# Attention with a gated MLP on one core: a new table of the order of instructions, with the activation table loaded by an early small exponential

## The chip, the cores and the metric

The kernel runs on one core of a Trainium2 chip. The metric is the device time of one execution in microseconds (us). All times of engines below are of one execution taken by the hardware profiler. PE is TensorE (its weight loads, which overlap its matmuls, are PEld), DVE is VectorE, ACT is ScalarE, POOL is GpSimd, SP is SyncE, which here only issues DMAs.

## What is computed

Attention of 4 batches with 12 heads, 448 positions and head dimension 64, with a causal mask and a softmax, and on its output, batch by batch, a gated MLP with a residual:

```python
scores = scale * np.matmul(q, k.transpose(0, 1, 3, 2))
scores = np.where(mask, -1000000000.0, scores)
scores = scores - np.max(scores, axis=-1, keepdims=True)
attn = np.exp(scores)
attn = attn / (np.sum(attn, axis=-1, keepdims=True) + 1e-09)
x = np.matmul(attn, v)                     # heads side by side: 448 x 768 per batch
h = x @ w_in                               # 768 x 1024
h = 0.5 * h * (1.0 + np.tanh(c * (h + 0.044715 * h ** 3)))
u, v = (h[..., :d_ff // 2], h[..., d_ff // 2:])
v_n = (v - mu) / np.sqrt(var + 1e-06) * g_ln
v_s = np.einsum('ts,bsd->btd', w_sg, v_n) + b_sg[None, :, None]
return x + (u * v_s) @ w_out
```

## The kernel before

**Attention** goes by pairs of heads, 24 pairs p, six to a batch. For each pair SP fetches queries and keys (tile qk, L424) and values (vraw, L516). PE makes the scores in two halves (`score(g)`, L431, tiles s, four PSUM banks for the two heads). DVE adds the mask and takes the row maxima (`mxs`, L446: s and ngm out of s and mask). ACT takes the exponentials with the maximum as bias and row sums on the side (L454: P out of s and ngm, ten instructions a pair, 64 to 448 columns wide). Three sets of P tiles, P_90, P_91 and P_92, and of row sums, sm_117 to sm_119, take turns over the pairs. Then P is transposed: for the first eight pairs on PE (L496, tiles tx and ty), with an eviction to B on ACT (L503) or DVE (L501); for the others on DVE (L484), with a DMA to B (L488). PE multiplies by the values (PV: L522, tile o), DVE scales by the reciprocal of the row sums (xt, L549; the reciprocal is L464 to L466 and goes through DRAM, L471 and L474), and ACT or POOL split the result into two rounded parts x (L555 to L560).

**MLP.** Per batch, PE makes the v half of the hidden layer in four chunks of positions (128, 128, 128 and 64 rows), then the u half, the product with w_sg over the four normalized chunks vn, and the product with w_out; all of these are L577, tiles m. The gelu is `gelu2` (L585 to L590, ACT and DVE in turn); the 64-row chunk has its two halves added first (L611, L613), then the normalization (L617 to L626) and the split into two parts (L630 and L631, for the 64-row chunk L635 on ACT and L636 on DVE, tile vn3). The gate is L669 to L676, the residual goes into res on POOL (L689) and is added to the last product on DVE (L702), from where SP stores it (L706, L710). In the last batch the last tile is added and stored in two halves of 224 columns.

**Weights** are fetched (L364, and L350 for w_sg) and split into two rounded parts on ACT, DVE and POOL (L366 to L374, L352, L353), beside the first batch. At the start seven matmuls on a cleared tile (L339) stand on PE.

**The order.** Each function records its operations with `od.add(engine, duration, function, reads, writes, ...)`. A table of 1883 numbers, `ORDER`, gives the order in which they are emitted; that sets the order of the instructions on each engine and on SP's queue, and in what turn buffers and banks go round. `plan` only makes sure that the table keeps the recorded dependencies; the durations and flags in the calls go into no instruction.

```python
    def plan(self):
        done = set()
        for n in ORDER:
            assert self.ops[n]["deps"] <= done
            done.add(n)
```

Operation 3 of the table is one exponential on a constant column (L330). The function of an exponential needs a table in ACT, and the load (ACT_TABLE_LOAD) is put before the first exponential that ACT is given; before the change that is one of the scores' (L454), and operation 3 stands after operation 1208.

Of the kernel before, what the change touches and what calls it, by code (L numbers as in the profile page):

```python
# [12 lines left out]
AF = mybir.ActivationFunctionType  # L13
ALU = mybir.AluOpType
# [211 lines left out]
def attention_gated_mlp(ctx: ExitStack, tc: tile.TileContext, qk, vP, w_in, g_ln, w_sgT, b_sg, w_out, out):  # L226
    nc = tc.nc
# [4 lines left out]
    DH = DF // 2  # L232
# [533 lines left out]
```

## Time and profile before

| | before |
|---|---|
| median of 3 runs | 339.13 us (338.38 to 340.37) |
| profiled execution, its own time | 337.29 us |
| its span, first to last instruction | 335.5 us |
| PE busy | 324.1 us |
| DVE busy | 251.0 us |
| ACT busy | 208.5 us |
| POOL busy | 175.9 us |
| mean granted clock of PE | 0.994 |

The profiled execution's own time is 1.84 us under the median of the runs, and its span 1.8 us under its own time. Busy times are sums over the whole span; where an engine stands still has to be read from windows of the span, from the timeline, and from what ended each pause, which the trace gives in brackets. PE's ends are modelled, so a busy PE is not PE at its peak. An instruction's duration overlaps the next one's on ACT and DVE by some tenth of a microsecond, so that the cost of one in a row of many is the time from its start to the next start.

### The profile page before, as it was taken

The numbers are of one execution on the slowest core, as the hardware profiler recorded it, in microseconds if no ns is written. First come the engines' busy times: TensorE is split into PE (matmuls) and PEld (weight loads), VectorE is DVE, ScalarE is ACT, GpSimd is POOL, SyncE is SP. The second block draws the span as 40 slices with busy tenths as digits, with TensorE's granted clock in tenths as the row PEclk, the third lists the DMA queues.
The fourth block names the chain that finished last, engine by engine and source line by source line (L and its number), as shares of the span: only waits on it lengthen the run. The fifth ranks groups of instructions, "written<-read, shape, count | busy, mean of one in ns | idle before, by whom it ended". The sixth has DMA issues, their size and how long they took to land.

```text
span 335.5 us, 7568 instructions
## 1 busy us (share of the span) xinstructions
PE 324.1 (97%) x2590; PEld 266.3 (79%) x2591; DVE 251.0 (75%) x762; ACT 208.5 (62%) x674; POOL 175.9 (52%) x225
## 2 busy tenths in 40 slices
PE   5699999999999999999999999999999999999995
PEld 3467678768887987878888978878989987889994
DVE  4899898999999888967977597889788531644613
ACT  1999999999894637666784526486674302355210
POOL 4258766888986964020535942014256824132691
PEclk9899999999999999999999999999999999999999
DMA  7889968595583688638747858739437440010004
GB/s 227 312 247 307 277 218 267 177 288 160 130 265 103 178 215 235 197 98 226 217 127 214 229 150 204 195 95 243 101 104 206 91 159 3 0 55 2 18 36 164
DMA packets 30965, 56.55 MB, mean 169 GB/s; under 512 B 6096, under 2 KB 15056, under 8 KB 30928
## 3 DMA queue, kind: packets, MB, share of 16 engines
q1 hardware_dynamic: 30928, 56.08, 57.5%
q8 instruction: 20, 0.33, 0.4%
q14 instruction: 17, 0.14, 0.1%
HBM read 33.39 MB, written 5.90 MB: 117 GB/s over the span
## 4 chain that ended last, share of the span: by engine, by line
PE 93%; ACT 4%; DMA 1%; DVE 1%; issue 0%; ACTq 0%; DVEq 0%
PE m L577 65%; PE o L522 13%; PE s L431 11%; ACT P L454 3%; PE ty L496 2%; PE tx L496 2%; DMA qk<-in_qk_dram 1%; PE m L339 0%; ACT L454 0%; ACT vn L366 0%; ACT B L503 0%; DVE s L446 0%; DVE res L702 0%; DVE ngm L446 0%; ACTq L454 0%
## 5 line engine op out<-in xcount | busy, mean ns | idle before, releaser
L454 ACT ACTIVATE P<-s,ngm 128x320 f32<-128x320 f32 (+3 forms) x240 | 102.7, 460 | 28.1 <-DVE ngm L446 19.7
L446 DVE CUSTOM_DVE_ANT_0 s<-s,mask 64x64 f32<-64x64 f32 (+3 forms) x192 | 77.6, 435 | 7.5 <-PE s L431 5.8
L577 PE MATMUL m<-win,x 128*128 128x512 f32 (+1 forms) x264 | 65.9, 399 | 0.0
L577 PE MATMUL m<-g,wout 128*128 128x448 f32 x288 | 61.1, 367 | 0.0
L577 PE MATMUL m<-x,win 128*128 128x448 f32 x288 | 61.1, 367 | 0.0
L577 PEld LDWEIGHTS m<-x,win 128*128 128x128 f32 x288 | 53.9, 188 | 5.0
L577 PEld LDWEIGHTS m<-g,wout 128*128 128x128 f32 x288 | 53.9, 188 | 5.0
L577 PEld LDWEIGHTS m<-win,x 128*128 128x128 f32 (+1 forms) x264 | 47.4, 183 | 11.7
L454 ACT ACTIVATION_READ_ACCUMULATOR P<-s,ngm 128x1 f32 (+1 forms) x240 | 55.1, 233 | 0.0
L431 PE MATMUL s<-qk 64*64 64x64 f32 (+5 forms) x768 | 45.2, 371 | 5.0 <-DMA qk<-in_qk_dram 4.4
L431 PEld LDWEIGHTS s<-qk 64*64 64x64 f32 x768 | 30.7, 139 | 21.6 <-issue 8.5
L522 PE MATMUL o<-B,vraw 128*64 128x64 f32 (+4 forms) x672 | 45.0, 291 | 0.0
L522 PEld LDWEIGHTS o<-B,vraw 128*64 128x64 f32 x672 | 32.8, 137 | 12.7 <-issue 4.5
L484 DVE STREAM_TRANSPOSE P<-P 128x1024 f32<-128x1024 f32 x32 | 38.2, 1224 | 0.7 <-DMA B<-P 0.6
L577 PE MATMUL m<-wsg,vn 128*128 128x448 f32 x176 | 38.3, 369 | 0.0
L621 POOL TENSOR_TENSOR mv<-mv,mhalf 128x1 f32<-128x1 f32 (+1 forms) x16 | 10.0, 626 | 49.0 <-DVE mv L619 40.7
L577 PEld LDWEIGHTS m<-wsg,vn 128*128 128x128 f32 x176 | 32.6, 188 | 3.6 <-DVE vn L636 0.4
L558 POOL TENSOR_TENSOR x<-xt,x 128x448 fp32r<-128x448 f32 x24 | 27.5, 1148 | 14.5 <-ACT x L557 14.2
L702 DVE TENSOR_TENSOR res<-m,res 128x448 f32<-128x448 f32 (+1 forms) x25 | 14.8, 603 | 23.2 <-PE m L577 15.2
L586 DVE SCALAR_TENSOR_TENSOR tmp<-tmp,m 128x448 f32<-128x448 f32 (+1 forms) x28 | 17.9, 640 | 16.2 <-ACT tmp L585 16.0
L673 POOL TENSOR_TENSOR tmp<-tmp,g 128x448 f32<-128x448 f32 x16 | 18.3, 1152 | 18.8 <-DVE tmp L669 18.8
L585 ACT ACTIVATE tmp<-m 128x448 f32<-128x448 f32 (+1 forms) x28 | 15.5, 562 | 20.3 <-PE m L577 19.2
(76 smaller groups left out, 410.8 us busy)
## 6 DMA issues: line engine op xcount, KB each, us to landing
B<-P SPq DMA_DIRECT2D x64, 256.0 KB
qk<-in_qk_dram SPq DMA_DIRECT2D x24, 448.0 KB
vn<-in_w_in_dram SPq DMA_DIRECT2D x12, 512.0 KB
vraw<-in_vP_dram SPq DMA_DIRECT2D x24, 256.0 KB
rb<-rd SPq DMA_DIRECT2D x24, 224.0 KB
out_dram<-res SPq DMA_DIRECT2D x9, 448.0 KB
g<-in_w_out_dram SPq DMA_DIRECT2D x16, 192.0 KB
out_dram<-res SPq DMA_DIRECT2D x5, 224.0 KB
```

Source lines behind the costliest of these rows:

```text
L431: nc.tensor.matmul(out=s[z][bk].t[64 * h:64 * h + 64, col:col + n], lhsT=qk_.t[r, 0, q0:q0 + 64], rhs=qk_.t[r, 1, k0:k0 + n], start=True, ...
L446: nc.vector.tensor_tensor_reduce(out=o, in0=i, in1=mk, scale=-0.125, scalar=3e38, op0=ALU.add, op1=ALU.min, accum_out=ngm[ib[z]][c][0:m])
L454: act(n, lambda c=c, m=m, k0=k0, n=n, bk=bk, col=col, off=off, kc=kc, i=i, z=z: nc.scalar.activation(out=P[i][0:m, off:off + n], in_=s[z][ ...
L484: dve(PW, lambda z=z: nc.vector.transpose(A[ia][:, :, :, z, :].rearrange("p g t k -> p t g k"), P[ib[z]]), Pk[z] + [kp], Ak, 1.105)
L496: nc.tensor.transpose(out, P[ib[z]][:, col:col + 128], ident)
L522: nc.tensor.matmul(out=dst(o.t[r]), lhsT=vr.t[:, c, r], rhs=src(z), start=first and n == 0, stop=last and n == len(lst) - 1)
L558: pool_tt(S, lambda: nc.gpsimd.tensor_tensor(out=y.t[:, S + 64:], in0=x.t, in1=f(y.t)[:, 0:S], op=ALU.subtract), [x, y], [(y, 1)])
L577: nc.tensor.matmul(out=ps.t[0:l().shape[1], 0:n], lhsT=l(), rhs=rr(), start=(k == 0), stop=(k == len(mms) - 1))
L585: act(n, lambda: nc.scalar.activation(out=z(), in_=h(), func=AF.Square), [ps], [t])
L586: dve(n, lambda: nc.vector.scalar_tensor_tensor(out=z(), in0=z(), scalar=1.0 / GC, in1=h(), op0=ALU.add, op1=ALU.mult), [ps], [t])
L673: pool_tt(S, lambda z=z, u=u: nc.gpsimd.tensor_tensor(out=z(), in0=z(), in1=u.t, op=ALU.mult), [u], [t])
L702: dve(hi - lo, lambda rr=rr, ps=ps, z=z, lo=lo, hi=hi: nc.vector.tensor_tensor(out=rr.t[:, z, lo:hi], in0=ps.t[:, lo:hi], in1=rr.t[:, z, l ...
```

## The change

The set of instructions stays the same. What differs is the order, and arguments that only the planner reads: the exponentials of the scores are recorded as readers of the early exponential on a constant (so that this stands ahead of all of them in any table that `plan` accepts), some durations are longer, and the 64-row gelu and L636 carry a flag `port`.

```diff
 ORDER = (
-    84, 85, 86, 1, 4, 0, 2, 89, 87, 90, 96, 88, 95, 98, 91, 92, 97, 99, 93, 94, 125, 126, 128, 127, 12, 18, 13, 103,
...
+    2, 4, 1, 0, 3, 84, 125, 332, 12, 18, 166, 330, 24, 85, 89, 87, 90, 96, 88, 95, 98, 97, 86, 91, 93, 92, 99, 94,
...
-    od.add("act", 0.2, lambda: nc.scalar.activation(out=pad[:, 0:1], in_=mhalf, func=AF.Exp), ["sm0"], ["table"])
+    od.add("act", 1.35, lambda: nc.scalar.activation(out=pad[:, 0:1], in_=mhalf, func=AF.Exp), ["sm0"], ["table"])
...
-                    [s[z][bk], ("ngm", i, c), kp, ks] + ([("P", i, k - 1)] if k == 1 else [("P", i, 2)] if k == 4 else []),
+                    [s[z][bk], ("ngm", i, c), kp, ks, "table"] + ([("P", i, k - 1)] if k == 1 else [("P", i, 2)] if k == 4 else []),
...
-        od.add("dve", 0.42, inv, sk + [ks], [("rT", ip)])
+        od.add("dve", 0.573, inv, sk + [ks], [("rT", ip)])
...
-            tensor=rd[ip].tensor, offset=rd[ip].offset, ap=[[512, 8], [0, 16], [1, S]])), [("rd", ip)], [rb], 320e3, dur=0.56)
+            tensor=rd[ip].tensor, offset=rd[ip].offset, ap=[[512, 8], [0, 16], [1, S]])), [("rd", ip)], [rb], 360e3, dur=0.56)
...
-    def gelu2(ps, m, n, dst=None):
+    def gelu2(ps, m, n, dst=None, port=False):
...
-                                                      op1=ALU.mult), [ps], [t])
+                                                      op1=ALU.mult), [ps], [t], port=port)
...
-                                                      op0=ALU.add, op1=ALU.mult), [ps, t], [d])
+                                                      op0=ALU.add, op1=ALU.mult), [ps, t], [d], port=port)
...
-                t, z = gelu2(hs, m, DH)
+                t, z = gelu2(hs, m, DH, port=True)
...
-            od.add("dve", 0.07, lambda mv=mv, m=m: nc.vector.tensor_scalar(
+            od.add("dve", 0.125, lambda mv=mv, m=m: nc.vector.tensor_scalar(
...
-                out=z(), in_=z(), func=AF.Identity, scale=mv.t[0:m, 1:2], bias=mv.t[0:m, 2:3]), [mv], [t], True)
+                out=z(), in_=z(), func=AF.Identity, scale=mv.t[0:m, 1:2], bias=mv.t[0:m, 2:3]), [mv], [t], True, 2)
...
-                                                                 op=ALU.subtract), [t, y], [(y, 1)])
+                                                                 op=ALU.subtract), [t, y], [(y, 1)], port=True)
```

ACT from its first instruction, before and after. A row is line, operation, output and inputs with their shape; P_90 and sm_117 belong to pair 0, P_91 and sm_118 to pair 1, ngm_93 to ngm_100 are pair 0's maxima:

```order
L454 ACT_TABLE_LOAD
L454 ACTIVATE P_90,sm_117<-s,ngm_100 128x448
L454 ACTIVATE P_90,sm_117<-s,ngm_96 128x448
L454 ACTIVATE P_90,sm_117<-s,ngm_97 64x64
L454 ACTIVATE P_90,sm_117<-s,ngm_93 64x64
L454 ACTIVATE P_90,sm_117<-s,ngm_95 128x320
L366 ACTIVATE vn<-vn 128x512
L454 ACTIVATE P_90,sm_117<-s,ngm_94 64x64
L454 ACTIVATE P_90,sm_117<-s,ngm_94 128x128
L454 ACTIVATE P_90,sm_117<-s,ngm_98 128x128
L454 ACTIVATE P_90,sm_117<-s,ngm_99 128x320
L454 ACTIVATE P_91,sm_118<-s,ngm_104 128x448
```

```order
L330 ACT_TABLE_LOAD
L330 ACTIVATE pad<-mhalf 128x1
L454 ACTIVATE P_90,sm_117<-s,ngm_100 128x448
L454 ACTIVATE P_90,sm_117<-s,ngm_96 128x448
L454 ACTIVATE P_90,sm_117<-s,ngm_97 64x64
L454 ACTIVATE P_90,sm_117<-s,ngm_93 64x64
L454 ACTIVATE P_90,sm_117<-s,ngm_95 128x320
L454 ACTIVATE P_90,sm_117<-s,ngm_94 128x128
L454 ACTIVATE P_90,sm_117<-s,ngm_94 64x64
L454 ACTIVATE P_90,sm_117<-s,ngm_99 128x320
L454 ACTIVATE P_90,sm_117<-s,ngm_98 128x128
L454 ACTIVATE P_90,sm_117<-s,ngm_98 64x64
```

The table load now belongs to the exponential of L330, on the column pad, and the ten exponentials of pair 0 follow without a weight split (L366) between them; in the whole of the first two pairs one L366 stands instead of two.

PE after the scores of pairs 0 and 1, before and after. The rows of L431 are the scores of pair 2, and ty and tx the transposes of pair 0's P (P_90) and, in after, of pair 1's (P_91):

```order
L496 MATMUL ty<-ident,P_90 128x128 x4
L431 MATMUL s<-qk 64x448 x2
L431 MATMUL s<-qk 64x384 x2
L431 MATMUL s<-qk 64x64 x2
L431 MATMUL s<-qk 64x320 x2
L431 MATMUL s<-qk 64x256 x2
L431 MATMUL s<-qk 64x128 x4
L431 MATMUL s<-qk 64x64 x2
L496 MATMUL ty<-ident,P_90 128x128 x4
L496 MATMUL tx<-ident,P_90 128x128 x8
```

```order
L496 MATMUL ty<-ident,P_90 128x128 x8
L431 MATMUL s<-qk 64x448 x2
L431 MATMUL s<-qk 64x384 x2
L431 MATMUL s<-qk 64x64 x2
L431 MATMUL s<-qk 64x320 x2
L431 MATMUL s<-qk 64x256 x2
L431 MATMUL s<-qk 64x128 x4
L431 MATMUL s<-qk 64x64 x2
L496 MATMUL tx<-ident,P_90 128x128 x8
L496 MATMUL tx<-ident,P_91 128x128 x8
```

All eight ty transposes of pair 0 moved ahead of pair 2's scores, and the tx transposes of both pairs follow in one piece. Behind these rows stand, before, ty, tx, ty, tx of pair 1 in fours and seven matmuls on the cleared tile; after, four ty, one such matmul, four ty and six of them. Then come pair 3's scores and PV of pairs 0 and 1 in both.

On POOL, the clearing of P, sm and wsg (ending with L325) moved from behind the making of ident and the masks to ahead of it. On SP, w_sg (L350) moved to the place after the first two qk, the first vraw moved behind, and the loads of the gain and the bias (L389, L390) moved from places 70 and 71 of the queue to its places 7 and 8.

DVE around L636 of the first batch (tile vn), before and after. L586 and L590 are steps of the gelu of the u half, L484 transposes of a later pair's P:

```order
L623 TENSOR_SCALAR mv<-mv 64x1
L586 SCALAR_TENSOR_TENSOR tmp<-tmp,m 128x448 x2
L464 TENSOR_REDUCE tot<-sm_117 128x8
L465 RECIPROCAL rs<-tot 128x8
L466 STREAM_TRANSPOSE rT_122<-rs 128x32
L636 TENSOR_TENSOR vn_1490<-tmp,vn_1490 64x512
L590 SCALAR_TENSOR_TENSOR g<-tmp,m 128x448
```

```order
L586 SCALAR_TENSOR_TENSOR tmp<-tmp,m 128x448
L484 STREAM_TRANSPOSE P_92<-P_90 128x8x4x32
L586 SCALAR_TENSOR_TENSOR tmp<-tmp,m 128x448
L623 TENSOR_SCALAR mv<-mv 64x1
L368 TENSOR_SCALAR g<-g 128x192
L549 TENSOR_TENSOR xt<-o,rb 128x448
L484 STREAM_TRANSPOSE P_92<-P_90 128x8x4x32
L636 TENSOR_TENSOR vn_1555<-tmp,vn_1555 64x512
L590 SCALAR_TENSOR_TENSOR g<-tmp,m 128x448 x2
```

The reciprocal (L464 to L466) moved further ahead, and two transposes and the xt sum (L549) of another pair now stand directly ahead of L636. On PE, PV of one more pair stands ahead of the product that reads this tile.

DVE at its end, before and after (L702 adds the last product to res):

```order
L702 TENSOR_TENSOR res<-m,res 128x448
L669 SCALAR_TENSOR_TENSOR tmp<-m,gcol,bB 128x448
L702 TENSOR_TENSOR res<-m,res 128x448 x2
L702 TENSOR_TENSOR res<-m,res 128x224 x2
L702 TENSOR_TENSOR res<-m,res 128x448 x3
```

```order
L669 SCALAR_TENSOR_TENSOR tmp<-m,gcol,bB 128x448
L590 SCALAR_TENSOR_TENSOR g<-tmp,m 128x448
L669 SCALAR_TENSOR_TENSOR tmp<-m,gcol,bB 128x448 x2
L702 TENSOR_TENSOR res<-m,res 128x448 x5
L702 TENSOR_TENSOR res<-m,res 128x224 x2
```

The tile that is added and stored in two halves moved to the last place; before, three whole tiles came behind it.

## Rows read from the trace of the kernel before

**Rows 1.** The page's busy times, and its chain by engine.

```profile
PE 324.1 (97%) x2590; PEld 266.3 (79%) x2591; DVE 251.0 (75%) x762; ACT 208.5 (62%) x674; POOL 175.9 (52%) x225
...
PE 93%; ACT 4%; DMA 1%; DVE 1%; issue 0%; ACTq 0%; DVEq 0%
```

**Rows 2.** Windows: length, then busy us per engine, granted clock, DMA share, GB/s.

```profile
10.00:15.00 5.00, 2.84 (x21) 1.75 (x25) 3.70 (x16) 5.00 (x22) 1.94 (x2) 0.91 0.98 377
15.00:20.00 5.00, 4.53 (x41) 3.93 (x33) 4.58 (x17) 5.00 (x22) 1.95 (x2) 0.75 0.59 186
...
80.00:100.00 20.00, 20.00 (x121) 17.36 (x120) 18.96 (x63) 17.45 (x54) 18.25 (x24) 1.00 0.59 168
...
330.00:336.00 6.00, 1.83 (x10) 1.35 (x8) 1.31 (x3) 0.00 (x0) 0.00 (x0) 0.91 0.39 147
```

**Rows 3.** Timeline of the start: start us, us, engine, line, operation, [idle before].

```profile
4.70 0.47 POOL L325 MEMSET wsg<- 64x448 f32 x1
...
5.94 0.23 DVE L446 CUSTOM_DVE_ANT_0 s<-s,mask 64x64 f32<-64x64 f32 x1 [3.88 <-PE s L431]
...
12.59 1.11 PE L431 MATMUL s<-qk 64*64 64x448 f32 x12 [0.46 <-DMA qk<-in_qk_dram]
...
14.36 2.06 PE L431 MATMUL s<-qk 64*64 64x320 f32 x20 [0.66 <-ACT P L454]
...
20.00 0.66 PE L496 MATMUL ty<-ident,P 128*128 128x128 f32 x4 [0.22 <-ACT B L503]
...
22.58 1.64 PE L431 MATMUL s<-qk 64*64 64x448 f32 x26
```

**Rows 4.** The chain that ended last, in order of time: PV of pairs 0 and 1.

```profile
24.33 3.71 PE o L522 x40
```

**Rows 5.** Timeline of ACT in the first ladder, accumulator reads left out.

```profile
7.07 1.28 ACT L454 ACT_TABLE_LOAD   x1 [7.07 <-DVE ngm L446]
8.37 0.63 ACT L454 ACTIVATE P<-s,ngm 128x448 f32<-128x448 f32 x1
...
8.99 0.62 ACT L454 ACTIVATE P<-s,ngm 128x448 f32<-128x448 f32 x1
...
9.61 0.30 ACT L454 ACTIVATE P<-s,ngm 64x64 f32<-64x64 f32 x1
...
9.89 0.30 ACT L454 ACTIVATE P<-s,ngm 64x64 f32<-64x64 f32 x1
...
10.18 0.52 ACT L454 ACTIVATE P<-s,ngm 128x320 f32<-128x320 f32 x1
...
10.69 0.68 ACT L366 ACTIVATE vn<-vn 128x512 f32<-128x512 f32 x1
11.24 0.32 ACT L454 ACTIVATE P<-s,ngm 64x64 f32<-64x64 f32 x1
...
14.16 0.34 ACT L454 ACTIVATE P<-s,ngm 64x64 f32<-64x64 f32 x1
...
19.27 1.63 ACT L503 ACTIVATE B<-tx 128x512 f32<-128x512 f32 x3
```

**Rows 6.** By source line: duration min/median/max ns, first and last start, form.

```profile
L590 DVE SCALAR_TENSOR_TENSOR tmp<-tmp x4: 674/1021/1477, 90.0 to 301.1; 64x512 f32<-64x512 f32 x4
...
L636 DVE TENSOR_TENSOR vn<-tmp,vn x4: 685/685/2120, 97.8 to 308.4; 64x512 fp32r<-64x512 f32 x4
```

**Rows 7.** Groups by form: count, busy us, mean ns, idle before and its releasers.

```profile
L484 DVE STREAM_TRANSPOSE P<-P 128x1024 f32<-128x1024 f32 x32 | 38.2, 1224 | 0.7 <-DMA B<-P 0.6
...
L577 PEld LDWEIGHTS m<-wsg,vn 128*128 128x128 f32 x176 | 32.6, 188 | 3.6 <-DVE vn L636 0.4 <-DVE g L590 0.4
...
L549 DVE TENSOR_TENSOR xt<-o,rb 128x448 f32<-128x448 f32 x24 | 14.6, 615 | 7.7 <-PE o L522 4.0 <-DMA rb<-rd 2.1 <-POOL x L555 0.7
```

**Rows 8.** Timeline of the tail: sums of the last output tiles.

```profile
327.64 0.69 DVE L702 TENSOR_TENSOR res<-m,res 128x224 f32<-128x224 f32 x2 [0.65 <-PE m L577]
...
331.87 0.62 DVE L702 TENSOR_TENSOR res<-m,res 128x448 f32<-128x448 f32 x1 [1.13 <-PE m L577]
```

178 rows, old and new, of the table ORDER are left out of this document.

## Prediction

> **What bounds the kernel now.** I read the page's engine totals and its chain first: PE is busy for 324.1 us of the span of 335.5, and the chain that ends last is PE for 93%, with 4% of ACT in it [rows 1]. So time can be won only where PE stands still, 335.5 − 324.1 = 11.4 us. The table of windows says where that is: PE has 2.84 of 5 us in 10:15 and 4.53 in 15:20, and 20.00 of 20 in a stretch as crowded as 80:100; ACT has 5.00 of 5 in both early windows [rows 2]. The bound is thus in two pieces. Up to about 24 us it is a ladder of max on DVE, exponential on ACT, transpose on PE and eviction on ACT or DVE, and ACT is the rung that never rests. After that it is PE's own work, some 307 us without a gap, and then the tail: last sum on DVE, one store.
>
> The timeline of the start shows the rungs. PE's second half of the scores of pair 2 starts at 14.36 and waits for an exponential; ty at 20.00 waits for an eviction on ACT; pair 3's scores stand from 22.58 [rows 3]; PV of pairs 0 and 1 begins at 24.33 [rows 4], and from there PE is full. I use that 24.33 as the mark: whatever the change does to it moves everything behind it, as long as PE stays full.
>
> **The early table load.** Before, ACT sits idle to 7.07, then loads its table for 1.28 us, and only then, at 8.37, does the first exponential [rows 5]. After, the tiny exponential of L330 stands first, so the load falls into idle time (it waits for a memset on DVE that is over before 2 us) and the first real exponential can start when its max is there, at 7.07. That is 8.37 − 7.07 = 1.30 us on ACT, at a place where nothing else was ready earlier. If nothing were late behind it, the mark would come 1.30 earlier; that is one end. The other end is 0: PE may wait there for something that ACT does not set.
>
> The Trainium skill ("ScalarE: Activation LUTs", section "What ACT_TABLE_LOAD costs") puts a switch of tables at about 1.28 us of load and 1.38 us of drain. By that the term would be 2.66. The trace shows the first half alone: the exponential starts 1.30 after the load did.
>
> **The new order of the start.** ACT now does all ten exponentials of pair 0, then those of pair 1, with one weight split (L366) between them instead of two. The exponential that frees the bank for the second half of pair 2's scores was ACT's at 14.16 before. Ahead of it stand now one more 448-wide, one 320-wide and one 64-wide exponential and one L366 less. From start to start these cost 8.99 − 8.37 = 0.62, 10.69 − 10.18 = 0.51, 9.89 − 9.61 = 0.28 and 11.24 − 10.69 = 0.55 [rows 5], so +0.86. It starts at 14.16 − 1.30 + 0.86 = 13.72 and ends near 14.0, and PE's scores start at about 13.9 to 14.1 instead of 14.36: 0.3 to 0.45 of the 1.30 is left there.
>
> Behind it the new order is shorter for ACT. The first tx eviction came at 19.27 [rows 5], behind all twenty exponentials of two pairs, one eviction, three L366 and one exponential of pair 2. Now two L366 (1.10) and that exponential (0.62) stand behind it: 1.72 less, with the 1.30 about 3.0, so ACT could take it at 16.3. But PE delivers tx only after the scores (2.0 long) and four matmuls at half clock (the 5 us from 15 had a granted clock of 0.75 [rows 2]), at about 17.0. So ACT idles some 0.7 to 1.0 us, which it did not before, and the eviction starts at 17.0 to 17.2. Then three evictions (0.48 each by 1.63 for three with the last one's tail), two L366 (1.10) and one more eviction, an exponential of 448 and one of 320 (1.13), and the last ty eviction: 17.1 + 1.45 + 1.10 + 0.48 + 1.13 + 0.5 = 21.8. That frees the bank for the second half of pair 3's scores, which take about 1.0; PV then starts at 22.9 to 23.5. I take 23.3: **the mark comes 1.0 earlier**. ACT's exponentials of pairs 2 and 3 are now tighter against PE's requests, and I give 0.1 back, so −0.9, with the ends −1.3 and 0.
>
> What else moves at the start is hidden. POOL now clears P, sm and wsg before it makes ident and the masks; that work ends at the same 4.70 + 0.47 = 5.17, and the first max that reads a mask starts at 5.94, because of the scores [rows 3]. The cover is 0.77. On SP pair 2's query transfer keeps its place, with wsg ahead of it in place of one V transfer; its landing gave 12.59 to PE [rows 3] and I leave it there. The row of the later bias and gain loads, now early, is beside transfers that nobody waits for.
>
> **The collisions on DVE.** The 64-row instructions L590 and L636 have two inputs in SBUF. Four L590 take between 674 and 1477 ns, and one L636 of four takes 2120 against 685 [rows 6]; both long ones lie beside POOL's tensor work. In all that is about 1.5 + 1.4 = 2.9 us of DVE. Removing all of it is worth to PE only what PE waited for it: of the idle time of its weight loads before the wsg products, 0.4 us is put down to L636 and 0.4 to L590 [rows 7], and PE itself shows 20.00 of 20 in 80:100 [rows 2]. So the term lies between −0.8 and 0 where collisions go, and I take 0, the row that is nearest to PE.
>
> **The tail.** The last group of PE is now the one whose sum is cut in two halves. Before: one sum of 0.62 and one store of 448 columns. After: 0.35 (0.69 for two [rows 8]), a store of half the size, then the second half's 0.35 and its store. The last store goes out at nearly the same moment (0.69 against 0.62) and has half the bytes. In 330:336 the DMA engines moved 147 GB/s × 6 us = 0.88 MB at a busy share of 0.39, 2.3 us [rows 2]; the last 224 KB are a quarter of it, 0.6, and half of that is saved less 0.07: −0.2, with ends −0.3 and +0.1.
>
> The remaining edits are durations and flags that the planner keeps and does not emit; by themselves they cost nothing.
>
> **The sum.** −0.9 − 0.2 + 0.1 (small stalls, next paragraph) = −1.0 against the profiled execution's own 337.29, so 336.3. Its time lies 1.84 under the median of the runs, and as a median I forecast 339.13 − 1.0 = **338.1 us**. About 1.7 us (0.5%) is what a measurement of this kernel can tell from no change, so this counts as the same.
>
> **Rivals.** *PE's clock holds (faster).* The granted clock of 0.75 in 15:20 means a quarter of 5 us, 1.25 us, of PE's work not done. If PE is busier before it, with eight transposes of pair 0 in a row at 11 to 12 us, and the clock stays at the upper of its two levels (2.4 GHz), tx comes earlier and ACT's new idle time shrinks: up to 1.25 more, 336.9. Against it: PE still waits for pair 2's query until 12.59, as before. I give it 0.2.
>
> *DVE late at the first batch's gate (slower).* The last wsg products of batch 0 need its L636. Directly ahead of it DVE had two L586 and the small steps of a reciprocal; now two transposes of P (1.22 each) and an xt sum (0.62) stand there too [rows 7], 3.06 us, while PE comes with one pair's PV more, half of 3.71 [rows 4], 1.85. So DVE is up to 1.2 tighter. PE comes another 1.0 earlier by the gain at the start, and one collision costs 0.8 (1.48 against 0.67). If DVE has no slack in hand when it comes to these steps, PE stands for 1.2 + 1.0 + 0.8 = 3.0: 341.1. For it: DVE is busy for 18.96 of 20 us there [rows 2], and PE's weight load waited 0.4 for that instruction already. Against: what DVE has shed (the reciprocal, the bias and gain scaling, which are earlier now) may be worth most of the 1.2, and three of four L636 were not hit. It decides from the point where DVE's lateness at L549 exceeds the products that PE still has ahead of the gate. I give it 0.17.
>
> *The start is not ACT's (no change).* Pair 2's landing at 12.59 and the half clock carry the ladder, ACT's lead turns into idle time, and the mark stays at about 24.1: 339.0. I give 0.13.
>
> *The collisions were what cost (a little faster).* If the waits of 0.8 go in full, 337.3. The Trainium skill ("SBUF — State Buffer", section "Who interferes with whom") calls the port pair that VectorE and GpSimd share an exclusive lock; the long rows fit that. This lies inside the forecast's own range.
>
> **How the numbers follow.** Forecast 0.5 (own range 337.3 to 339.0), clock 0.2, gate 0.17, no change 0.13. Faster by over 0.5% means under 337.4: nearly all of the clock's 0.2 and 0.05 of the forecast's, 0.25. Slower by over 0.5% means over 340.8: most of the gate's, 0.14, and a little for places I have not priced, 0.16. The range reaches down to 336.7, which takes in the clock, and up to 340.6, half of the gate.
>
> **What would show it.** In the profile after: the table load ahead of 3 us and the first exponential at about 7.1; ACT with a gap near 16.5 to 17.1; PV of pair 0 at about 23.3; PE full from there; the last two sums 224 wide and the end 0.2 nearer to PE's last matmul. I am wrong if the mark is within 0.3 of 24.33 or before 22.6, or if PE shows a gap over 0.5 us between 60 and 310 us, above all before the wsg products of batch 0.

## The result and the profile after

The changed kernel takes **342.93 us** (median of 4 runs, 342.24 to 343.54) against 338.94 (338.38 to 340.37) for the kernel before on the same chip: a ratio of 1.0114, 95% interval 1.0086 to 1.0142, slower by 4.0 us. The forecast was 338.1 with a range to 340.6. It was wrong, and on the side that I had given least. The profiled execution of after has a time of 342.74 and a span of 341.0, against 337.29 and 335.5.

The page of after, busy times and chain by engine; it answers to [rows 1]:

```profile
PE 328.0 (96%) x2591; PEld 266.2 (78%) x2591; DVE 256.5 (75%) x762; ACT 208.4 (61%) x674; POOL 174.9 (51%) x225
...
PE 79%; DVE 10%; ACT 8%; issue 1%; DMA 1%; DVEq 0%; ACTq 0%
```

The set of instructions is the same, yet DVE is busy for 256.5 us instead of 251.0, and it has come into the chain with 10%. The windows say when (columns as in [rows 2]; the last two numbers are DMA's busy share and GB/s). First two of before, then those of after:

```profile
50.00:60.00 10.00, 10.00 (x98) 8.19 (x95) 8.97 (x33) 9.95 (x37) 6.29 (x8) 1.00 0.84 269
60.00:80.00 20.00, 20.00 (x186) 14.54 (x185) 19.65 (x68) 19.32 (x67) 16.39 (x22) 1.00 0.78 238
```

```profile
10.00:15.00 5.00, 3.99 (x46) 2.24 (x40) 4.53 (x18) 5.00 (x22) 1.25 (x2) 1.00 1.04 378
15.00:20.00 5.00, 4.91 (x43) 3.44 (x40) 4.52 (x23) 5.00 (x19) 0.71 (x1) 1.00 0.77 257
...
50.00:60.00 10.00, 8.90 (x79) 6.25 (x78) 9.79 (x35) 8.75 (x35) 9.08 (x11) 1.00 0.82 279
60.00:80.00 20.00, 19.11 (x148) 13.35 (x147) 19.97 (x51) 16.97 (x57) 15.54 (x22) 1.00 0.68 196
80.00:100.00 20.00, 18.20 (x134) 14.93 (x132) 19.81 (x61) 15.81 (x48) 13.00 (x17) 1.00 0.77 221
100.00:120.00 20.00, 20.00 (x142) 17.32 (x143) 19.73 (x53) 12.28 (x33) 17.33 (x26) 1.00 0.54 156
```

The start is better than forecast: PE has 3.99 and 4.91 of 5 where it had 2.84 and 4.53, at a granted clock of 1.00 in both. Between 50 and 100 us it is worse: PE had 10.00 of 10, 20.00 of 20 and, in 80:100, 20.00 of 20 [rows 2]; now it has 8.90, 19.11 and 18.20, with DVE at 9.79, 19.97 and 19.81. The start, in the timeline of after:

```profile
0.73 1.28 ACT L330 ACT_TABLE_LOAD   x1 [0.73 <-PEq L755]
...
7.09 0.63 ACT L454 ACTIVATE P<-s,ngm 128x448 f32<-128x448 f32 x1 [4.79 <-DVE ngm L446]
```

and PE's PV of pairs 0 and 1, in the timeline of PE alone, before and after; it answers to [rows 4]:

```profile
24.26 2.94 PE L522 MATMUL o<-B,vraw 128*64 128x448 f32 x22
```

```profile
22.04 3.70 PE L522 MATMUL o<-B,vraw 128*64 128x448 f32 x40
```

PE begins with PV at 22.04 instead of 24.26, so the lead is 2.2 us. By the end it had become a lag of 341.0 − 335.5 = 5.5: between these two profiled executions **7.7 us were lost behind the start**. But the one of before is a short one, 337.29 against a median of 338.94. By the medians the loss is 4.0 + 2.2 = **6.2 us**, and that is the figure to explain. To place it I added up, for each group of matmuls in the order's table, how much longer its step to the next one was than the usual step of its kind. From 30 to 100 us this is 9.5 us in after and 2.8 in before; behind 100 us 3.5 and 3.0. Nearly all of the loss that the two traces show lies in the first batch, between 30 and 100 us, where the weights are still being split.

What DVE did there, by source line up to 110 us (min/median/max ns, first and last start). First L368 and L370 of the kernel before, then of after:

```profile
L368 DVE TENSOR_SCALAR g<-g x16: 244/256/711, 45.3 to 105.9; 128x192 int32<-128x192 int32 x16
L368 DVE TENSOR_SCALAR vn<-vn x12: 409/424/450, 9.4 to 83.8; 128x512 int32<-128x512 int32 x12
...
L370 DVE SCALAR_TENSOR_TENSOR g<-g x16: 315/345/1311, 45.6 to 106.8; 128x192 int32<-128x192 int32 x16
L370 DVE SCALAR_TENSOR_TENSOR vn<-vn x12: 674/692/701, 11.4 to 84.3; 128x512 int32<-128x512 int32 x12
```

```profile
L368 DVE TENSOR_SCALAR g<-g x16: 245/284/1191, 44.5 to 104.7; 128x192 int32<-128x192 int32 x16
L368 DVE TENSOR_SCALAR vn<-vn x12: 389/426/1546, 11.6 to 87.6; 128x512 int32<-128x512 int32 x12
...
L370 DVE SCALAR_TENSOR_TENSOR g<-g x16: 317/349/1476, 61.9 to 109.5; 128x192 int32<-128x192 int32 x16
L370 DVE SCALAR_TENSOR_TENSOR vn<-vn x12: 673/770/1668, 12.8 to 90.1; 128x512 int32<-128x512 int32 x12
```

The shortest are the same, the longest have grown by 0.2 to 1.1 us. One of them beside POOL, in the timelines of the two engines in after:

```profile
78.44 1.39 POOL L374 TENSOR_TENSOR win<-vn,win 128x512 fp32r<-128x512 f32 x1
```

```profile
78.57 1.48 DVE L370 SCALAR_TENSOR_TENSOR g<-g 128x192 int32<-128x192 int32 x1
```

POOL's subtraction starts 0.13 ahead and ends at 79.83; DVE's instruction, 0.32 by itself, ends at 80.05, only 0.22 behind POOL's end, so most of its work came when POOL was done. Counted over the whole span, 16 of DVE's instructions in after are over 0.2 us longer than the shortest of their form, 12.0 us in sum, all of them between 41 and 99 us and each beside an instruction of POOL; in before there are 7, 4.9 us in sum, and only four of them, 2.5 us, ahead of 100 us. Of the 12.0 us L368 has 5.0, L370 4.9, and the 64-row L586 and L590 the rest. The growth of 12.0 − 4.9 = 7.1 us covers the 5.5 by which DVE's busy time grew; the other instructions must be 1.6 shorter in sum, which I have not traced.

How it reaches PE is told by the chain of after around 95 us:

```profile
90.82 0.87 DVE g L368 x3
...
91.98 1.73 DVE tmp L586
...
95.65 1.47 DVE tmp L590
...
98.66 1.26 ACT P L454 x6
...
99.97 1.99 PE o L522 x32
```

DVE has a queue of weight splits, gelu steps and row maxima; the maxima come late, so the exponentials, so PV. The tail, in the timeline of after, answers to [rows 8]:

```profile
337.22 0.69 DVE L702 TENSOR_TENSOR res<-m,res 128x224 f32<-128x224 f32 x2 [1.17 <-PE m L577]
```

From there to the end of the span are 341.0 − 337.22 = 3.78 us; before, from the whole tile's sum, 335.5 − 331.87 = 3.63.

### The profile page after: what moved, and what is told of

The parts are those of the page before. It is cut to its first block, busy times and chain, and to the rows that moved or that the text cites. A ratio compares the mean times of both kernels' runs of the same rounds, so it can differ in the third digit from the quotient of the medians.

```text
span 341.0 us, 7561 instructions
## 1 busy us (share of the span) xinstructions
PE 328.0 (96%) x2591; PEld 266.2 (78%) x2591; DVE 256.5 (75%) x762; ACT 208.4 (61%) x674; POOL 174.9 (51%) x225
## 4 chain that ended last, share of the span: by engine, by line
PE 79%; DVE 10%; ACT 8%; issue 1%; DMA 1%; DVEq 0%; ACTq 0%
PE m L577 57%; PE o L522 11%; PE s L431 9%; ACT P L454 5%; DVE s L446 3%; ACT B L503 2%; DVE g L368 1%; DVE vn L370 1%; PE ty L496 1%; DMA qk<-in_qk_dram 1%; ACT vn L366 1%; DVE tmp L586 1%; PE tx L496 1%; DVE P L484 1%; DVE tmp L590 1%
## 5 line engine op out<-in xcount | busy, mean ns | idle before, releaser
L454 ACT ACTIVATE P<-s,ngm 64x64 f32<-64x64 f32 (+3 forms) x240 | 100.9, 450 | 43.1 <-DVE ngm L446 27.3
L446 DVE CUSTOM_DVE_ANT_0 s<-s,mask 64x64 f32<-64x64 f32 (+3 forms) x192 | 76.8, 439 | 11.7 <-PE s L431 10.2
L577 PE MATMUL m<-g,wout 128*128 128x448 f32 x288 | 61.8, 368 | 0.0
L454 ACT ACTIVATION_READ_ACCUMULATOR P<-s,ngm 128x1 f32 (+1 forms) x240 | 53.0, 225 | 0.0
L431 PE MATMUL s<-qk 64*64 64x128 f32 (+5 forms) x768 | 47.6, 376 | 4.7 <-DMA qk<-in_qk_dram 3.9
L431 PEld LDWEIGHTS s<-qk 64*64 64x64 f32 x768 | 30.9, 140 | 23.7 <-issue 8.0
L522 PE MATMUL o<-B,vraw 128*64 128x64 f32 (+4 forms) x672 | 45.8, 291 | 1.5 <-ACT P L454 1.3
L484 DVE STREAM_TRANSPOSE P<-P 128x1024 f32<-128x1024 f32 x32 | 38.7, 1227 | 7.5 <-DMA B<-P 6.7
L621 POOL TENSOR_TENSOR mv<-mv,mhalf 128x1 f32<-128x1 f32 (+1 forms) x16 | 8.9, 555 | 50.1 <-DVE mv L619 50.1
L558 POOL TENSOR_TENSOR x<-xt,x 128x448 fp32r<-128x448 f32 x24 | 27.9, 1166 | 6.2 <-ACT x L557 5.6
L702 DVE TENSOR_TENSOR res<-m,res 128x448 f32<-128x448 f32 (+1 forms) x25 | 14.4, 593 | 21.0 <-PE m L577 20.1
L689 POOL TENSOR_TENSOR res<-x 128x448 f32<-128x448 f32 x24 | 28.2, 1191 | 2.5 <-DMA out_dram<-res 2.5
L588 ACT ACTIVATE tmp<-tmp 128x448 f32<-128x448 f32 (+2 forms) x32 | 19.1, 601 | 16.8 <-DVE tmp L586 16.8
L446 DVE DVE_READ_ACCUMULATOR2_ANT ngm<- 64x1 f32 (+1 forms) x192 | 25.9, 135 | 0.0
```

Source lines behind the costliest of these rows:

```text
L431: nc.tensor.matmul(out=s[z][bk].t[64 * h:64 * h + 64, col:col + n], lhsT=qk_.t[r, 0, q0:q0 + 64], rhs=qk_.t[r, 1, k0:k0 + n], start=True, ...
L446: nc.vector.tensor_tensor_reduce(out=o, in0=i, in1=mk, scale=-0.125, scalar=3e38, op0=ALU.add, op1=ALU.min, accum_out=ngm[ib[z]][c][0:m])
L454: act(n, lambda c=c, m=m, k0=k0, n=n, bk=bk, col=col, off=off, kc=kc, i=i, z=z: nc.scalar.activation(out=P[i][0:m, off:off + n], in_=s[z][ ...
L484: dve(PW, lambda z=z: nc.vector.transpose(A[ia][:, :, :, z, :].rearrange("p g t k -> p t g k"), P[ib[z]]), Pk[z] + [kp], Ak, 1.105)
L522: nc.tensor.matmul(out=dst(o.t[r]), lhsT=vr.t[:, c, r], rhs=src(z), start=first and n == 0, stop=last and n == len(lst) - 1)
L558: pool_tt(S, lambda: nc.gpsimd.tensor_tensor(out=y.t[:, S + 64:], in0=x.t, in1=f(y.t)[:, 0:S], op=ALU.subtract), [x, y], [(y, 1)])
```

## Experiments

**The theory**: the early table load and the new start are good; the new order of the first batch lays DVE's weight splits beside POOL's instructions, DVE waits these out, and PE waits for DVE. A collision is here a DVE instruction beside one of POOL, over 0.2 us longer than the shortest of its form. **The rivals**: a start that is earlier makes DVE late at the gates of batch 0 in any order, collisions or not; the collisions come from the shift of the start and not from the order; DVE's own order, or POOL's results, are what PE waits for.

### The early load alone

The order table of the kernel before with one number moved:

```diff
-    84, 85, 86, 1, 4, 0, 2, 89, 87, 90, ...
+    84, 85, 86, 1, 3, 4, 0, 2, 89, 87, 90, ...
```

> The kernel before with one number of its order table moved: the small exponential of L330, and with it the table load, stands first on ACT; everything else keeps its order. Theory (the loss lies in DVE instructions that wait for POOL between 40 and 100 us; the early load itself is good): PV of pair 0 starts 1.0 to 2.2 us before 24.33, nothing else is lost, median 336.8 to 338.0. Rival (any earlier start only makes DVE late at the gates of batch 0, whatever the order): the start is earlier and the gain is given back or more, 339 to 341.

Measured: 337.74 us (10 runs, 336.59 to 338.83) against 338.92, ratio 0.9967 (0.9946 to 0.9988). A window of it, and PV in PE's timeline:

```profile
15.00:20.00 5.00, 3.48 (x26) 2.77 (x27) 4.46 (x18) 5.00 (x18) 2.86 (x4) 1.00 0.69 219
```

```profile
23.01 1.85 PE L522 MATMUL o<-B,vraw 128*64 128x448 f32 x16
```

PV starts 24.26 − 23.01 = 1.25 earlier, and 1.2 us are left of it in the median. DVE's long instructions are the same seven with 4.9 us, at places that moved by some 0.7 us. The rival, that any earlier start is given back, falls for this lead of 1.25; a lead of 2.2 in the old order is tried below. This version is faster than both kernels.

### The new order with the late load

The changed kernel with operation 3 put back behind operation 1208:

```diff
-    2, 4, 1, 0, 3, 84, 125, ...
+    2, 4, 1, 0, 84, 125, ...
...
-    1207, 1208, 1106, ...
+    1207, 1208, 3, 1106, ...
```

> The changed kernel with the small exponential put back behind operation 1208, so that the table load stands ahead of the first exponential of the scores again; the rest of the new order stays. Theory (DVE with its waits for POOL is what PE waits for from 40 to 100 us): the start loses 1.3 to 2.2 us, but DVE is so late there that most of it is absorbed: 342.5 to 344. Rival (the start's lead is what brings DVE and POOL out of step, the collisions come from the shift): the long L368 and L370 become few, 339 to 341.

Measured: 343.79 us (4 runs, 343.52 to 345.05), ratio to before 1.0154 (1.0117 to 1.0192). PV starts at 23.22, 1.18 later than in after, and the median is 0.9 later. The time is within the theory's range, but the theory had most of the start's loss absorbed, and most of it came through. The collisions are all there, 17 with 12.3 us, shifted with the start. A window, PV, and one pair of instructions of it, DVE and POOL:

```profile
15.00:20.00 5.00, 4.95 (x46) 4.40 (x46) 3.53 (x21) 5.00 (x19) 1.44 (x2) 0.84 0.60 209
```

```profile
23.22 3.70 PE L522 MATMUL o<-B,vraw 128*64 128x448 f32 x40
```

```profile
79.72 1.48 DVE L370 SCALAR_TENSOR_TENSOR g<-g 128x192 int32<-128x192 int32 x1
```

```profile
79.59 1.39 POOL L374 TENSOR_TENSOR win<-vn,win 128x512 fp32r<-128x512 f32 x1
```

It is the pair of after, 1.15 us later and with the same 0.13 between the two starts. So a shift of the start by 1.2 us leaves the collisions nearly as they were: they come from the order, not from the moment, and the rival of the shift falls. With the run above the start is a square: PV at 24.26 and 23.22 with the late load, 23.01 and 22.04 with the early one. **The load is worth 1.2 and the new order of the start 1.0**, each whatever the other is. These are four single executions, but the corners repeat: PV starts between 21.9 and 22.1 in all seven runs with the new start and the early load, and between 24.2 and 24.8 in all five with the old start and the late one.

### POOL without its long reads

In both kernels five kinds of POOL work (L353, L374, L558, L631, L689) keep their two inputs for 8 columns only; the rest of each output is cleared. The low parts of weights and activations and the residual are left out by that.

```diff
+    def tt8(out, in0, in1, op):
+        nc.gpsimd.tensor_tensor(out=out[:, 0:8], in0=in0[:, 0:8], in1=in1[:, 0:8], op=op)
+        nc.gpsimd.memset(f(out)[:, 8:], 0.0)
...
-        pool_tt(n, lambda: nc.gpsimd.tensor_tensor(out=dst(1), in0=f(lo()), in1=f(dst(0)), op=ALU.subtract),
+        pool_tt(n, lambda: tt8(out=dst(1), in0=f(lo()), in1=f(dst(0)), op=ALU.subtract),
```

> The changed kernel with five kinds of POOL work cut to 8 columns with two inputs and a clearing of the rest (L353, L374, L558, L631, L689: the low parts of weights and activations and the residual are left out), so that POOL's instructions beside DVE are short. Theory (collisions cost the 6 to 7 us that PE stands more between 35 and 100 us): DVE loses its 8 to 12 us of long L368, L370, L586 and L590, PE's gaps there go, 335.5 to 337.5, and it is faster than the same cut of the kernel before by 1 to 2.5 us. Rival (the order of DVE itself makes PE wait): the gaps stay, 341 or more, and it is slower than the same cut of the kernel before by 3 to 5.

> The kernel before with the same cut of POOL's work (the low parts of weights and activations and the residual are left out). Both theories: little to gain, since PE stood still for about 2.5 us between 35 and 100 us and for 2 us after it: 337 to 338.8. It is the mark against which the cut of the changed kernel is read.

Measured: 336.47 us with the new order (5 runs, 335.71 to 337.01; ratio to before 0.9919, 0.9889 to 0.9948) and 337.35 with the old one (10 runs, 336.84 to 338.25; 0.9961, 0.9946 to 0.9977). The new order gains 6.5 us by the cut, the old one 1.6, and the new one is now the faster of the two, by 0.9 (a little under the 1 to 2.5 that was expected). DVE's splits (now L372 and L374) and two windows in the cut of the new order:

```profile
L372 DVE TENSOR_SCALAR g<-g x16: 222/250/751, 43.6 to 96.9; 128x192 int32<-128x192 int32 x16
L372 DVE TENSOR_SCALAR vn<-vn x12: 389/418/428, 11.5 to 82.8; 128x512 int32<-128x512 int32 x12
...
L374 DVE SCALAR_TENSOR_TENSOR g<-g x16: 317/348/354, 58.2 to 102.5; 128x192 int32<-128x192 int32 x16
L374 DVE SCALAR_TENSOR_TENSOR vn<-vn x12: 648/688/706, 12.8 to 85.4; 128x512 int32<-128x512 int32 x12
```

```profile
60.00:80.00 20.00, 20.00 (x160) 15.07 (x158) 17.95 (x55) 17.51 (x59) 13.55 (x36) 1.00 0.76 219
80.00:100.00 20.00, 19.98 (x162) 16.66 (x162) 18.64 (x61) 18.05 (x59) 11.12 (x38) 1.00 0.63 178
```

No long L374 is left, and of the one-input L372 there are four, 1.6 us in sum; PE is full where it had 19.11 and 18.20. DVE's order is the same as in after, so that order alone does not make PE wait there. But POOL was also done sooner, which would help by itself. So the clearing was then made twice, which gives POOL its time back:

```diff
-        nc.gpsimd.memset(f(out)[:, 8:], 0.0)
+        for _ in range(2):
+            nc.gpsimd.memset(f(out)[:, 8:], 0.0)
```

> As the changed kernel with POOL's work cut to 8 columns and a clearing, but the clearing is made twice, so that POOL is busy about as long per operation as with the real work (0.2 + 2 x 0.47 against 1.15 us, 0.25 + 2 x 0.52 against 1.33); the same parts are left out of the result. In the run with one clearing, DVE instructions beside a clearing kept their short times. Theory (what costs is that a DVE instruction waits out a POOL instruction that reads, not POOL's time): 335.8 to 337.5, with hardly any long L368 or L370. Rival (POOL's results come later, PE and DVE wait for them): 340 or more.

> The kernel before with the same: POOL as long, without its reads, the same parts of the result left out. Both theories: 337 to 338.8; the mark for the run beside it.

Measured: 337.24 us with the new order (10 runs, 335.88 to 338.61; 0.9961, 0.9939 to 0.9983) and 337.49 with the old one (10 runs, 336.72 to 338.63; 0.9959, 0.9934 to 0.9985). One kind of the clearing, L368 and L370 (now L373 and L375), and three windows, in the run with the new order:

```profile
L335 POOL MEMSET win<- 128x504 f32 x24 | 12.6, 525 | 0.7
```

```profile
L373 DVE TENSOR_SCALAR g<-g x16: 244/339/741, 44.6 to 97.6; 128x192 int32<-128x192 int32 x16
L373 DVE TENSOR_SCALAR vn<-vn x12: 386/425/765, 11.6 to 83.3; 128x512 int32<-128x512 int32 x12
...
L375 DVE SCALAR_TENSOR_TENSOR g<-g x16: 318/347/800, 60.1 to 102.9; 128x192 int32<-128x192 int32 x16
L375 DVE SCALAR_TENSOR_TENSOR vn<-vn x12: 649/688/772, 12.9 to 86.1; 128x512 int32<-128x512 int32 x12
```

```profile
35.00:60.00 25.00, 24.92 (x262) 18.09 (x259) 23.62 (x95) 25.00 (x96) 20.96 (x53) 1.00 0.87 274
60.00:80.00 20.00, 20.00 (x160) 15.15 (x159) 19.62 (x59) 17.78 (x59) 16.64 (x49) 1.00 0.77 221
80.00:100.00 20.00, 20.00 (x165) 16.94 (x164) 19.37 (x62) 18.39 (x59) 15.54 (x48) 1.00 0.64 191
```

From 30 to 100 us POOL is busy for 56.97 us in this run against 54.79 in after, and from 35 us on PE is full but for 0.08 us. Against the kernel before beside each, after is 4.0 slower and this run 1.3 faster: 5.3 us for POOL's reads in the new order, and 1.0 in the old one. What costs is mainly the waiting of DVE behind POOL's reads, and not POOL's time or the age of its results. **This shows the cause of 4.2 of the 6.2 us** (5.28 − 1.04).

The rest stays open. Without the reads the new order is faster than the old one by 0.9 with one clearing and by 0.25 with two, though its start is 2.2 us ahead, so some 1.3 to 2.0 us are still lost. Nine DVE instructions over 0.2 us too long are left in the run with two clearings, 3.2 us in sum, against two with 0.8 in the old order; the order of the later batches, below, is another candidate.

### Splices of the two orders

Four runs take one order up to a point of the table and the other for what is left.

> The new order up to PV of pair 10 (866 numbers, about 100 us), then the order of the kernel before. Theory: the loss is all there, 341.8 to 343.5. Rival (the loss needs the later batches too): 340.5 or less.

> The kernel before's order up to PV of pair 10 (882 numbers, about 100 us), then the new order with its tail. Theory (all of the loss lies ahead of that point, the rest of the new order is neither better nor worse by more than 0.7): 338.3 to 339.6. Rival (the new order also loses in the later batches): 340 or more.

Measured: the new order up to about 100 us and the old one behind it 343.14 us (4 runs, 343.10 to 344.12; 1.0148, 1.0126 to 1.0170); the old one up to there and the new one behind it 340.01 (10 runs, 338.79 to 342.61; 1.0048, 1.0023 to 1.0073). So the loss is there with the new order up to that point alone, as expected. The second is 0.4 above its upper bound and just meets what its rival said, 340 or more: the new order of the later batches, or the seam, costs about 1.6 us. The traces of before and after give the later part only 0.5, and which it is stays open.

> The changed kernel's order up to the first PV (its first 117 numbers, the early table load among them), then the order of the kernel before for all that is left. Theory (the new start is worth 2.2 us at the first PV, the loss lies in the new order of the middle, where DVE waits for POOL): PV starts near 22.0, DVE has about 5 us of waits for POOL as in the kernel before and not 12, median 336.0 to 337.5, and it beats the kernel before. Rival (a start that is 2.2 us earlier makes DVE late at the gates of batch 0 in any order): 338.5 or more, with PE gaps between 35 and 100 us of over 4 us.

> The kernel before's order up to its first PV (148 numbers, with the late table load), then the new order. Theory: PV near 24.3, the 10 to 12 us of waits of DVE for POOL are there again between 42 and 100 us, 343 to 345.5. Rival (the collisions belong to the shift of the start): 338 to 340.

Measured: the new start with the old rest 342.26 us (6 runs, 341.25 to 344.19; 1.0121, 1.0094 to 1.0149); the old start with the new rest 351.5 (4 runs, 350.2 to 352.5; 1.0386, 1.0359 to 1.0413). Both miss, and neither tells what it was meant to: a new gap stands at the seam. The first has the time of its rival (338.5 or more), but not its gaps: PE stands for 1.3 us between 35 and 100 us, not over 4. In it, PV starts at 22.09, and then PE stands for 3.4 us before a ty because ACT waits 4.05 us for the transfer of a weight; DVE's long instructions are 10 with 6.7 us. In the second PE stands for 5.3 us, until 36 us, for an xt sum; its collisions are 14 with 9.8 us. I took SP's queue for the cause and kept it whole in the old order:

> As the run with the new order up to the first PV and the old one behind it, but SP's queue keeps the whole order of the kernel before, so that at the seam ACT finds the weights that the old order lets it split there. PE, ACT, DVE and POOL have the new start. Theory (the 3.4 us for which PE stood at that seam were the queue's; the new start is worth its 2.2 us, and the old middle has few collisions): PV near 22.0, no gap over 1 us between 22 and 35, 336.0 to 337.7. Rival (ACT has no room to keep such a lead, whatever the queue): a gap of 2 us or more before 60 us, 338.5 or more.

> The same with POOL's order of the kernel before as well, so that only PE, ACT and DVE have the new start. Theory: as the run beside it within 0.6, 336.0 to 337.9, with the same collisions of DVE and POOL as in the kernel before. Rival: 338.5 or more.

Measured: 341.7 us (6 runs, 341.11 to 342.88; 1.0095, 1.0067 to 1.0122) and 342.61 (6 runs, 342.12 to 343.44; 1.0115, 1.0088 to 1.0142). The theory on the queue falls, and both times are the rival's, that ACT has no room for such a lead whatever the queue. In the first of the two, ACT's timeline and a window:

```profile
26.76 0.66 ACT L366 ACTIVATE vn<-vn 128x512 f32<-128x512 f32 x1 [2.79 <-DMA vn<-in_w_in_dram]
```

```profile
25.00:30.00 5.00, 2.13 (x27) 1.55 (x24) 3.54 (x12) 3.24 (x16) 2.52 (x4) 1.00 0.88 280
```

ACT still waits 2.79 us for a weight's transfer. The new start splits fewer weights by then: up to 24 us ACT had begun four splits (L366) here and five in before. The tiles that the transfers fill then come free later. That the tiles hold up the transfer is argued, not shown; no run gave them another buffer. What the runs do show is that the two halves of these orders could not be joined at this point without a new wait, and that the new start's 1.0 us could not be had with the old middle in these ways. Whether any order keeps the whole lead of 2.2 us is open: no run kept more than 1.2.

## Why the prediction was wrong, point by point

**What bounds the kernel.** PE's own work behind 24 us and a ladder on ACT ahead of it: right for the kernel before. What I did not draw from it: with DVE at 18.96 of 20 us in 80:100 [rows 2] there was room for about 1 us more of DVE in such a stretch. Of the 9.5 us that the collisions grew by ahead of 100 us (12.0 − 2.5), 4.2 to 4.9 reached the time.

**The step that failed: the collisions on DVE.** I priced them at "between −0.8 and 0" and took 0. Two errors are in it. I looked for long instructions only where the flag `port` was new, at L590 and L636 [rows 6], and let the mean of the weight splits stand for each of them. The row of L370 in before shows 315 to 1311 ns: it had been hit as well. And I let the term end at 0 above, because the flag names what a planner should avoid; that an order can have more of them than before was not in the range. It did: 12.0 us against 4.9. Measured by the cut with POOL's time kept, each against the kernel before beside it, the term is +5.3 in the new order (342.93 − 338.94 = +4.0, and 337.24 − 338.53 = −1.3) and +1.0 in the old one (338.53 − 337.49): **+4.2 where I had 0**, and +4.9 by the cut with one clearing.

The Trainium skill ("SBUF — State Buffer", section "Who interferes with whom") names both forms: an instruction with two SBUF inputs beside GpSimd's reads, and a tensor_scalar in a mode that uses both ports. The traces agree that both were held up (L370 at 1.48 instead of 0.32, L368 at up to 1.55 instead of 0.39); that L368 runs in such a mode no run shows apart from this. I had used the section for one rival and one kind of instruction; read through against DVE's whole list in batch 0, it bears on 56 instructions there, 28 of each line.

**The start.** The mark was forecast 1.0 earlier and came 2.2 earlier. At 22.04 it is past my own sign of being wrong (before 22.6); the other sign, a PE gap over 0.5 us, came as well (1.03 us ahead of a PV at 99.97). The load's 1.30 was right (1.18 and 1.25). The new order was taken as a loss of 0.3 and is a gain of 1.0. ACT came to its first tx eviction at 16.28, as the count of 16.3 had it, but I held PE's tx back to 17.0. The second half of pair 2's scores began at 13.43 (I had 13.9 to 14.1) and tx at 15.15, at a granted clock of 1.00, so ACT's idle time of 0.7 to 1.0 did not come; ACT has 5.00 of 5 in both windows. Pair 2's first scores began at 11.83, not at the 12.59 that I kept; but in five other runs with the new start they began at 12.0 to 12.5, and PV came within 0.1 us of this one, so that was not what made the gain. The clock that I held for likely to fall did not: the faster rival's condition came about. What it gave no run separates: with the early load alone it held as well, for a gain of 1.25 that the load's 1.30 covers, and in the new order with the late load it fell to 0.82 and 0.84, and the order still gained 1.0.

**The tail.** −0.2 forecast; 3.78 us against 3.63 from the last sum's start to the end, +0.15. Half the bytes did not bring the end nearer in these two executions. The +0.1 for small stalls in the sum has no row behind it.

**The gate of batch 0.** This rival was the right place and sign (DVE late in the first batch, slower), and its 341.1 was the nearest number, but its mechanism was another, so the nearness is in part luck: L636 kept PE's weight loads for 0.2 us, less than the 0.4 before. In after PE waited for exponentials and gelu steps ahead of it.

**The chances.** Slower by over 0.5% had 0.16. The profile had three signs for more: DVE at 18.96 of 20 us, instructions that were hit already, and a new order of just these instructions.

## What to carry to other kernels

When an order is changed, list for each engine that is nearly full in a stretch (DVE had 18.96 of 20 us here) which of its instructions can be held up by a neighbour, and look at the shortest and the longest of each form, never at the mean. A gain ahead of such a stretch lasts only if the stretch does not grow; here one number of the table (the early load) gave 1.2 us for nothing, while a new order of all 1883, with the same early load in it, gained 2.2 at the start and lost 6.2 behind it. To tell a lock from a lack of time, keep the neighbour as long but take away what it locks.

## What the runs showed of the hardware that I had not expected

- A one-input L368 (128x192, 0.25 us) beside POOL took up to 1.19 us, and POOL's casts hold it up as well: at 77.96 one of 128x512 took 0.69 instead of 0.39 beside L373. Beside POOL's clearings the two-input L370 kept its 0.35 and 0.69 at the median, while the median of the one-input form (128x192) was 0.34 where the clearing was made twice and 0.25 where it was made once.
- PE's granted clock stayed at 1.00, the upper of its two levels, through 10 to 20 us in every run with the early load (eight kernels), and fell below it in every run with the late one: 0.75 in 15:20 before, 0.84 in the new order with the late load, 0.50 in the cut of the kernel before. In 10:15 PE was busy for 2.87 of 5 us with the early load alone, at 1.00, and for 3.73 in the new order with the late load, at 0.82; why the clock held is open. In the splice that kept SP's queue, where PE had 2.13 of 5 us in 25:30, it fell to 0.66 in the 5 us behind that.
